# Two PSUM pairs kept through the late groups and the tail, single banks for the last chain, pieces of x W between the real and the imaginary products, ten units through GpSimd

## The chip, the cores and the metric

The kernel runs on one core of a Trainium2 chip. The core has TensorE (PE, matrix products, writing only to PSUM), VectorE (DVE) and ScalarE (ACT), which read PSUM and SBUF, GpSimd (POOL), which works on SBUF, and SyncE (SP), which here only issues DMAs. PSUM has eight banks of 2 KB per partition; one fp32 row of 512 fills a bank. The metric is the device time of one execution in microseconds (us); lower is better.

## The reference

Two layers in a row. The first is a linear attention with exponential features (8 batches, 8 heads, 576 tokens, 64 columns per head); its output, heads side by side, is x (8 x 576 x 512). The second mixes the lowest 64 frequencies of x along the sequence with complex weights for each frequency and ends in a product with w_ch:

```python
X = np.fft.rfft(x, axis=1)
Xr, Xi = (np.real(X[:, :n_modes]), np.imag(X[:, :n_modes]))
Yr = np.einsum('bmd,mde->bme', Xr, w_r) - np.einsum('bmd,mde->bme', Xi, w_i)
Yi = np.einsum('bmd,mde->bme', Xr, w_i) + np.einsum('bmd,mde->bme', Xi, w_r)
Y[:, :n_modes] = Yr + 1j * Yi
y = np.fft.irfft(Y, n=S, axis=1)
u = x + y
return (u + np.maximum(u @ w_ch, 0.0)).astype(np.float32)
```

w_r and w_i are 64 x 512 x 512 each in fp32, 134 MB together; they are read once.

## The kernel before, in words

**Stages.** The attention runs in steps n (the loop at L578). Beside it, and after it, the weights stream in: 32 groups k, each with a tile wr and a tile wi (128 x 8 x 512 in bf16, three buffers of each, tags w0 and w1), and each tile by two DMAs of 512 KB on POOL's queue (L166), which convert fp32 to bf16. A DMA for group k + 3 needs the buffer of group k, so POOL waits there for the matmuls that read it. mode_mm (L410) makes the product of one group with the spectrum XT, sixteen matmuls into psY: eight with wr, eight with wi. mode_sum (L443) adds psY to Yacc, and for the last eight groups, k = 24 to 31, writes the sum as yst in bf16.

**The late loop** (L834) covers k = 21 to 30, after the attention. Because u @ w_ch = x @ w_ch + y @ w_ch and y is an inverse transform (matrix CI) of Y, the kernel forms x @ w_ch ahead of time, "x W" below, in 17 pieces of two 128-token chunks: flip_x (L679) transposes two chunks into pt (PSUM tag tr) and copies them to sT on DVE; times_w (L690) does eight matmuls into psW (tag pW, two buffers), which ACT copies into xw. A group that has yst is transposed into ptY (tag tr) and copied into sY (transposed, L825). After every second such group by_batch (L734) multiplies sY by w_ch (mm_z) and by the identity (mm_r) into two psZY tiles of two banks each (tags T0, T1): z in the first bank, r in the second. Eight copies (four on ACT, four on DVE, L740) move these by batch into zall and yall; regroup(n) issues n pairs of them. reordered (L704) permutes chunk pairs of xs_all in place for "late" units, two matmuls and an ACT copy each, through T0 and T1. A table, plan (L831), says whether a second piece is done between the real and the imaginary product of a group; one piece always follows the imaginary product.

**The last group.** Here the PSUM pool psumL is closed and psumT opened (L870), with four pairs T0 to T3. Group 31's product goes to T1; unit 0's sums are started between its two halves; then come yst in two halves, two transposes and sY, mm_z and mm_r for h = 0 and h = 1 (T0, T1), and the move into rows 96 to 127 of zall and yall: batch 0 directly (L888, L889), the seven others through st (L893, L894) and DMAs on SP and POOL (L896).

**The units.** The output is made in 18 units of two chunks each, in the order of seq (L699): (batch, chunk, late). A unit adds x W and CI @ z in psB (add_xw L770, add_z L777), ACT takes its relu into the output tile o (L779), psA collects x and CI @ y (add_x L785, spec L791), and DVE adds psA to o (L793). A late unit leaves out the two matmuls for x; POOL adds x from xs_all instead (L796). Units with c = 4 are half units: they take the last chunk of four batches, and their two DMAs write from 64 partitions each, out of Yacc. The first and the last unit are cut in two. Even units use the pair T2, T3, odd ones T0, T1. SP issues the output DMAs (L916) in an order that is worked out from the list done (L899): a unit's number, for late ones a count of when POOL will be through. SP's queue runs in order, so a DMA that waits holds those behind it. An output tile takes a buffer of wr or wi.

All of this stands in manual_schedule blocks: on each engine the instructions run in the order of the program text.

Of the kernel before, what the change touches and what calls it, by code (L numbers as in the profile page):

```python
# [10 lines left out]
F32 = mybir.dt.float32  # L11
# [9 lines left out]
DMODEL = 512  # L21
# [5 lines left out]
def kernel(  # L27
# [639 lines left out]

    psum_cm = tc.tile_pool(name="psumL", bufs=1, space=bass.MemoryType.PSUM)
# [21 lines left out]
    def times_w():  # L690
        i, sT = ahead.pop(0)
        for x in range(2):
# [6 lines left out]
    seq = [(0, 0, 0), (0, 2, 1), (1, 0, 1), (1, 2, 1), (4, 0, 1), (4, 2, 1),  # L699
           (5, 0, 0), (5, 2, 1), (2, 0, 1), (0, 4, 0), (2, 2, 1), (6, 0, 1),  # L700
           (6, 2, 0), (3, 0, 1), (3, 2, 1), (2, 4, 0), (7, 0, 0), (7, 2, 0)]
    reorder = sorted(b * NCH + c for b, c, late in seq if late)

    def reordered(tag):  # L704
# [4 lines left out]
        ps = psum.tile([128, 2, DMODEL], F32, name="psX", tag=tag)  # L709
# [8 lines left out]
    def mm_z(ps, cols, h):  # L718
        for dc in range(4):
            for j in range(4):  # L720
                nc.tensor.matmul(ps[32 * j:32 * j + 32, 0, :], lhsT=cols[dc][:, j + 4 * h::8],
                                 rhs=wchb[:, dc, :], start=(dc == 0), stop=(dc == 3))

    def mm_r(ps, cols, h):
        for dc in range(4):
            for j in range(4):
                nc.tensor.matmul(
                    ps[32 * j:32 * j + 32, 1, dc * 128:(dc + 1) * 128],
                    lhsT=cols[dc][:, j + 4 * h::8], rhs=ident_b, start=True, stop=True)

    def zy_psum():
        return [psum.tile([128, 2, DMODEL], F32, name="psZY", tag=f"T{h}") for h in range(2)]

    def by_batch(sY, P):  # L734
        cols = columns(sY)
        ps = zy_psum()
        rows = slice(32 * P, 32 * P + 32)

# [3 lines left out]
        for h in range(2):  # L742
            mm_z(ps[h], cols, h)
            mm_r(ps[h], cols, h)
# [21 lines left out]
    def add_xw(u):  # L766
        u["psB"] = ps = psum.tile([128, 2, DMODEL], F32, name="psB", tag=u["tags"][0])
# [13 lines left out]
    def add_x(u):  # L781
        u["psA"] = ps = psum.tile([128, 2, DMODEL], F32, name="psA", tag=u["tags"][1])
# [17 lines left out]
    for n, (b, c, late) in enumerate(seq):  # L800
        u = dict(b=b, c=c, late=late == 1, half=c == 4, cut=n in (0, len(seq) - 1), n=n,
                 tags=("T2", "T3") if n % 2 == 0 else ("T0", "T1"))
# [28 lines left out]
    plan = {21: 2, 22: 2, 23: 2, 24: 2, 25: 1, 26: 2, 27: 1, 28: 1, 29: 1, 30: 2}  # L831
    with tc.manual_schedule():
        flip_x()
        for k in range(k_out, 31):  # L834
            gi = groups[k][1]
            while k_in < min(k + NW, 32):
                weights(k_in)
                k_in += 1
            issue_weights()
            psY = mode_mm(k, "pY", (0,))  # L840
            if plan[k] > 1:
                times_w()
                if todo:
                    flip_x()
            regroup(2)
            mode_mm(k, "pY", (1,), psY)
            yst = mode_sum(k, psY, pb)
            regroup(99)
            times_w()
# [5 lines left out]
            if todo:  # L855
                flip_x()
# [3 lines left out]
            if gi % 2 == 0 or k < 24:  # L860
# [3 lines left out]
        assert not todo and not copies  # L864
        while ahead:
            times_w()
        while reorder:
            reordered("T0")

    psum_cm.__exit__(None, None, None)  # L870
    psum = ctx.enter_context(tc.tile_pool(name="psumT", bufs=1, space=bass.MemoryType.PSUM))

    with tc.manual_schedule():
        psY = mode_mm(31, "T1", (0,))
# [3 lines left out]
        mode_mm(31, "T1", (1,), psY)  # L878
        yst = mode_sum(31, psY, pb)
        pt = psum.tile([128, 4, 128], BF16, name="ptY", tag="T0")  # L880
        transposed(yst, sY, 7, (((0, 2), pt[:, 0:2, :]), ((2, 4), pt[:, 2:4, :])))
        cols = columns(sY)
        ps = zy_psum()
        st = [pb.tile([128, 2, DMODEL], BF16, name=f"st{h}", bufs=1) for h in range(2)]
        rows = slice(96, 128)
        mm_z(ps[0], cols, 0)
        mm_r(ps[0], cols, 0)
        nc.scalar.copy(zall[rows, 0, :], ps[0][0:32, 0, :])  # L888
        nc.vector.tensor_copy(yall[rows, 0, :], ps[0][0:32, 1, :])  # L889
        mm_z(ps[1], cols, 1)  # L890
        mm_r(ps[1], cols, 1)
        for h in range(2):
            nc.scalar.copy(st[h][:, 0, :], ps[h][:, 0, :])  # L893
            nc.vector.tensor_copy(st[h][:, 1, :], ps[h][:, 1, :])  # L894
            for j in range(1 - h, 4):
                (nc.sync if j < 2 else nc.gpsimd).dma_start(  # L896
                    zy[rows, :, j + 4 * h, :], st[h][32 * j:32 * j + 32])

        done, free = [], 0  # L899
# [47 lines left out]
```

## Time and profile before

| | |
|---|---|
| time, median of 3 runs | 453.44 us (453.36 to 454.44) |
| the profiled execution | 454.95 us, its span 453.0 us |
| TensorE busy / weight loads | 309.5 us (68%) / 207.3 us (46%) |
| DVE, ACT, POOL busy | 300.7 us (66%), 273.0 us (60%), 221.0 us (49%) |
| HBM read / written | 163.64 MB / 9.44 MB |
| weight DMAs (POOL's queue) | 128 of 512 KB, median 18.6 and 19.0 us from issue to landing |
| output DMAs (SP's queue) | 14 of 512 KB, 8 of 256 KB, median 3.6 to 4.3 us |
| mean granted TensorE clock | 0.875 of full speed |

The shares are means over stages with different limits. The late loop runs from about 318 to 409 us, the last group's chain to 418, the units to 445, and the last output lands near 452. In a row of the timeline the columns are start, length, engine, line, operation, output <- input, shapes, count, and in brackets the idle time before it with what ended it. In a row of the windows they are the stretch, its length, the busy us of PE, PEld, DVE, ACT and POOL (count), the granted clock, the busy share of the 16 DMA engines (transfers that convert types count above 1) and GB/s.

### The profile page before, as it was taken

How to read it: one execution, taken by the hardware profiler on the slowest of the kernel's cores; microseconds unless marked ns; L12 is line 12 of the kernel's file. 1: busy time of each engine (PE TensorE's matmuls, PEld its weight loads, DVE VectorE, ACT ScalarE, POOL GpSimd, SP SyncE). 2: the span in 40 equal slices, each digit the busy share in tenths (PEclk: the TensorE clock that was granted, in tenths of full speed). 3: DMA queues.
4: the chain of work that ended last, by engine and by line, in shares of the span. 5: the costliest groups of instructions: out<-in, count | busy, mean ns of one | idle time of the engine just before them, and what ended most of it. 6: DMA issues, size and time to landing. Idle time of an engine off the chain costs nothing.

```text
span 453.0 us, 11872 instructions
## 1 busy us (share of the span) xinstructions
PE 309.5 (68%) x4979; PEld 207.3 (46%) x4997; DVE 300.7 (66%) x419; ACT 273.0 (60%) x570; POOL 221.0 (49%) x303
## 2 busy tenths in 40 slices
PE   3475677666566578666666577666999856677991
PEld 2364556555455466554454454444444424244440
DVE  6578879988599878988585587753222626263882
ACT  4575777767475588787575586662356625153761
POOL 3965557565565746644564464442232222100992
PEclk9997979988696668999698688887799989899998
DMA  6999999999999999999999999999999999990698
GB/s 177 208 229 219 207 192 218 227 218 218 206 232 221 223 232 220 222 228 221 222 232 212 221 234 211 211 211 211 211 211 211 211 211 211 211 189 15 228 351 298
DMA packets 60917, 97.83 MB, mean 216 GB/s; under 512 B 3904, under 2 KB 28800, under 8 KB 60864
## 3 DMA queue, kind: packets, MB, share of 16 engines
q0 software_dynamic: 51920, 76.75, 94.3%
q1 hardware_dynamic: 8784, 20.26, 13.1%
q8 instruction: 39, 0.64, 0.5%
q14 instruction: 14, 0.11, 0.1%
q10 hardware_dynamic: 160, 0.07, 0.1%
HBM read 163.64 MB, written 9.44 MB: 382 GB/s over the span
## 4 chain that ended last, share of the span: by engine, by line
DVE 27%; PE 26%; DMA 22%; ACT 9%; issue 6%; POOL 6%; SPq 1%; DVEq 0%; ACTq 0%; POOLq 0%
DMA wi<-in_moe_w_i_dram 21%; DVE mkq L245 9%; DVE xs_all L348 5%; DVE nd L334 4%; PE psW L695 3%; DVE tB L327 3%; ACT AA L252 3%; PE psNB L317 2%; PE ptr L196 2%; POOL vaug L282 2%; PE psY L435 2%; PE kvz L298 2%; ACT AA L256 2%; PE psB L770 2%; PE psWe L406 2%
## 5 line engine op out<-in xcount | busy, mean ns | idle before, releaser
L282 POOL TENSOR_TENSOR vaug<-vn,ee 128x576 bf16<-128x576 f32 x64 | 72.9, 1163 | 37.1 <-ACT ee L267 30.6
L166 POOL DMA_DIRECT2D wr<-in_moe_w_r_dram x48 | 29.7, 621 | 75.5 <-PE psY L435 30.0
L252 ACT ACTIVATE AA<-psT 128x1024 bf16<-128x1024 f32 x64 | 62.0, 1021 | 7.0 <-PE psT L220 6.3
L274 ACT ACTIVATE e<-mkq 64x4 f32<-64x4 f32 (+1 forms) x128 | 26.3, 206 | 65.4 <-DVE mkq L245 62.9
L256 ACT ACTIVATE AA<-psk 128x1024 bf16<-128x1024 f32 x64 | 61.3, 1008 | 0.0
L166 POOL DMA_DIRECT2D wi<-in_moe_w_i_dram x48 | 30.0, 628 | 35.8 <-DMA wi<-in_moe_w_i_dram 15.3
L202 DVE COPY kT<-ptr 128x640 bf16<-128x640 bf16 x32 | 15.7, 492 | 43.4 <-PE ptr L196 43.4
L298 PE MATMUL kvz<-vaug,AA 64*128 64x65 bf16 x1152 | 28.5, 207 | 22.0 <-POOL vaug L287 19.9
L697 ACT CAST xw<-psW 128x512 bf16<-128x512 f32 x34 | 19.8, 586 | 36.1 <-PE psW L695 31.8
L245 DVE TENSOR_REDUCE mkq<-psq 128x8 f32<-128x1024 f32 x32 | 38.9, 1217 | 0.8 <-PE psq L211 0.4
L245 DVE TENSOR_REDUCE mkq<-psk 128x8 f32<-128x1024 f32 x32 | 38.8, 1211 | 1.1 <-PE psk L211 1.0
L695 PE MATMUL psW<-wchb,sT 128*128 128x512 bf16 x126 | 35.4, 415 | 2.4 <-DVE sT L687 1.6
L298 PEld LDWEIGHTS <-AA 64*128 64x128 bf16 x1152 | 24.8, 105 | 26.1 <-issue 21.3
L348 DVE TENSOR_TENSOR xs_all<-nd,rden 128x640 bf16<-128x640 f32 x32 | 35.7, 1116 | 1.1
L220 PE MATMUL psT<-qT,w 64*128 64x512 bf16 x64 | 14.1, 428 | 31.6 <-DVE mkq L245 31.5
L317 PEld LDWEIGHTS <-AA 128*128 128x128 bf16 x640 | 31.5, 115 | 7.8 <-issue 7.4
L327 DVE TENSOR_TENSOR tB<-psNB,e 128x650 f32<-128x650 f32 x32 | 26.7, 833 | 9.7 <-PE psNB L317 8.9
L196 PE MATMUL ptr<-ident_b,k 128*128 128x128 bf16 x160 | 18.6, 265 | 16.8 <-DVE qT L202 14.8
L687 DVE COPY sT<-pt 128x1024 bf16<-128x1024 bf16 x17 | 11.8, 692 | 27.5 <-PE pt L684 23.6
L334 DVE TENSOR_TENSOR nd<-psNA,tB 128x650 f32<-128x650 f32 x32 | 26.7, 835 | 3.8 <-DVE tB L327 0.5
L435 PEld LDWEIGHTS <-XT 128*32 128x32 bf16 x384 | 15.0, 174 | 27.7 <-issue 14.3
L435 PE MATMUL psY<-wi,XT 128*32 128x512 bf16 x192 | 16.2, 408 | 11.2 <-DMA wi<-in_moe_w_i_dram 11.2
(136 smaller groups left out, 733.7 us busy)
## 6 DMA issues: line engine op xcount, KB each, us to landing
wr<-in_moe_w_r_dram POOLq DMA_DIRECT2D x64, 512.0 KB, 18.6
wi<-in_moe_w_i_dram POOLq DMA_DIRECT2D x64, 512.0 KB, 19.0
out_dram<-of SPq DMA_DIRECT2D x14, 512.0 KB, 4.1
vn<-in_v_dram SPq DMA_DIRECT2D x24, 288.0 KB, 6.2
q<-in_q_dram POOLq DMA_DIRECT2D x12, 288.0 KB, 18.0
k<-in_k_dram POOLq DMA_DIRECT2D x12, 288.0 KB, 16.2
vn<-in_v_dram SPq DMA_DIRECT2D x16, 144.0 KB, 4.8
out_dram<-of SPq DMA_DIRECT2D x4, 256.0 KB, 3.6
```

The source lines that it names most:

```text
L166: nc.gpsimd.dma_start(t.rearrange("p (m i) e -> p m (i e)", i=2), w[8 * gi + y:8 * gi + 8:2, g * 128:(g + 1) * 128, :].rearrange("m (p i) ...
L245: nc.vector.tensor_reduce(out=o, in_=i, axis=AX.X, op=ALU.max, apply_absolute_value=True)
L252: nc.scalar.activation(AA[:, 0, ab, 0:1024].rearrange("f (x j p) -> f j x p", j=2, p=64), st["psT"].rearrange("f j (x p) -> f j x p", p=64 ...
L256: nc.scalar.activation(AA[:, 1, ab, 0:1024].rearrange("p (c j f) -> p j c f", c=4, j=2), st["psk"], ACT.Exp, scale=sc)
L282: nc.gpsimd.tensor_tensor(out=vaug[:, ab, :, 0:64], in0=st["v"], in1=ee[:, ab, :].unsqueeze(2).to_broadcast([128, 9, D_]), op=ALU.mult,)
L298: nc.tensor.matmul(kvz[:, hh, ab * 65:(ab + 1) * 65], lhsT=AA[r, 1, ab, 128 * j:128 * j + 128], rhs=vaug[r, ab, j, :], start=(j == 0), sto ...
L317: nc.tensor.matmul(p[:, hh, 65 * c:65 * c + 65], lhsT=AA[:, 0, ab, x:x + 128], rhs=kvzF[:, hh, ab * 65:(ab + 1) * 65], start=True, stop=True,)
L327: nc.vector.tensor_tensor(out=tB, in0=st["psNB"], in1=e2.unsqueeze(3).to_broadcast([128, 2, NCH, 65]), op=ALU.mult,)
L334: nc.vector.tensor_tensor(out=nd, in0=st["psNA"], in1=st["tB"], op=ALU.add)
L348: nc.vector.tensor_tensor(out=xo, in0=nd[:, :, :, 0:64], in1=rden.to_broadcast([128, 2, NCH, 64]), op=ALU.mult,)
L435: nc.tensor.matmul(psY[32 * j:32 * j + 32, :], lhsT=XT[:, 16 + 32 * ri:48 + 32 * ri, 32 * i + 4 * gi + j], rhs=wt[ri][:, 2 * j + i, :], st ...
L695: nc.tensor.matmul(ps, lhsT=sT[:, x, dc, :], rhs=wchb[:, dc, :], start=(dc == 0), stop=(dc == 3))
```

## The change

Four things, all from the late loop on.

The pairs T0 and T1 move into a pool of their own, psumA, which is opened with psumL and stays open to the end. psumL then has the single banks tr, pY and two of pW. The close and reopen ahead of group 31 is gone; psumL is closed and psumT (T2, T3) opened ahead of unit 1. Even units use T0, T1 from psumA, odd ones T2, T3.

Group 31 takes its product in pY and its transposes in tr. Its z and r each get a tile of one bank: pW and pW for h = 0, pY and tr for h = 1. Batches 0 and 1 are moved directly (four copies instead of two), the other six by DMA.

In the late loop each group has a piece (times_w, then flip_x if any is left) between its real and its imaginary product, and all waiting copies of by_batch follow there. A second piece behind the imaginary product is done for k in pieces_behind.

seq has a new order with ten late units instead of eleven, and the order of the output DMAs counts 4 for a unit, 3 for a late one, 6 for a half one, and 5 for an add on POOL.

```diff
+    psumA = ctx.enter_context(tc.tile_pool(name="psumA", bufs=1, space=bass.MemoryType.PSUM))
     psum_cm = tc.tile_pool(name="psumL", bufs=1, space=bass.MemoryType.PSUM)
...
-    seq = [(0, 0, 0), (0, 2, 1), (1, 0, 1), (1, 2, 1), (4, 0, 1), (4, 2, 1),
-           (5, 0, 0), (5, 2, 1), (2, 0, 1), (0, 4, 0), (2, 2, 1), (6, 0, 1),
-           (6, 2, 0), (3, 0, 1), (3, 2, 1), (2, 4, 0), (7, 0, 0), (7, 2, 0)]
+    seq = [(0, 0, 0), (0, 2, 1), (1, 0, 1), (1, 2, 0), (2, 0, 1), (2, 2, 1),
+           (3, 0, 0), (3, 2, 1), (4, 0, 1), (0, 4, 0), (4, 2, 1), (5, 0, 1),
+           (5, 2, 0), (6, 0, 1), (6, 2, 1), (7, 0, 0), (2, 4, 0), (7, 2, 0)]
...
-                 tags=("T2", "T3") if n % 2 == 0 else ("T0", "T1"))
+                 tags=("T0", "T1") if n % 2 == 0 else ("T2", "T3"),
+                 pool=(lambda: psumA) if n % 2 == 0 else (lambda: psum))
...
-    plan = {21: 2, 22: 2, 23: 2, 24: 2, 25: 1, 26: 2, 27: 1, 28: 1, 29: 1, 30: 2}
+    def modes_of(k, part, psY=None):
+        if part == 0:
+            while issue["k"] < min(k + NW, 32):
+                weights(issue["k"])
+                issue["k"] += 1
+            issue_weights()
+        return mode_mm(k, "pY", (part,), psY)
+
+    def piece():
+        times_w()
+        if todo:
+            flip_x()
+
+    issue = dict(k=k_in)
+    pieces_behind = (21, 22, 24, 26, 28, 30)
...
-            psY = mode_mm(k, "pY", (0,))
-            if plan[k] > 1:
-                times_w()
-                if todo:
-                    flip_x()
-            regroup(2)
-            mode_mm(k, "pY", (1,), psY)
-            yst = mode_sum(k, psY, pb)
-            regroup(99)
-            times_w()
+            psY = modes_of(k, 0)
+            piece()
+            regroup(99)
+            modes_of(k, 1, psY)
+            yst = mode_sum(k, psY, pb)
+            if k in pieces_behind:
+                times_w()
...
-            if todo:
+            if k in pieces_behind and todo:
                 flip_x()
...
-    psum_cm.__exit__(None, None, None)
-    psum = ctx.enter_context(tc.tile_pool(name="psumT", bufs=1, space=bass.MemoryType.PSUM))
...
-        psY = mode_mm(31, "T1", (0,))
+        psY = modes_of(31, 0)
         u0 = units[0]
         add_xw(u0)
         add_x(u0)
-        mode_mm(31, "T1", (1,), psY)
+        modes_of(31, 1, psY)
...
-        mm_z(ps[0], cols, 0)
-        mm_r(ps[0], cols, 0)
-        nc.scalar.copy(zall[rows, 0, :], ps[0][0:32, 0, :])
-        nc.vector.tensor_copy(yall[rows, 0, :], ps[0][0:32, 1, :])
-        mm_z(ps[1], cols, 1)
-        mm_r(ps[1], cols, 1)
-        for h in range(2):
-            nc.scalar.copy(st[h][:, 0, :], ps[h][:, 0, :])
-            nc.vector.tensor_copy(st[h][:, 1, :], ps[h][:, 1, :])
-            for j in range(1 - h, 4):
-                (nc.sync if j < 2 else nc.gpsimd).dma_start(
+        for h, tags in ((0, ("pW", "pW")), (1, ("pY", "tr"))):
+            z, r = [psum.tile([128, DMODEL], F32, name="ps" + "ZR"[x], tag=tags[x],
+                              bufs=2 if h == 0 else 1) for x in range(2)]
+            mm_z(z, cols, h)
+            mm_r(r, cols, h)
+            for j in range(2 - 2 * h):
+                nc.scalar.copy(zall[rows, j, :], z[32 * j:32 * j + 32])
+                nc.vector.tensor_copy(yall[rows, j, :], r[32 * j:32 * j + 32])
+            nc.scalar.copy(st[h][:, 0, :], z)
+            nc.vector.tensor_copy(st[h][:, 1, :], r)
+            for j in range(2 - 2 * h, 4):
+                (nc.sync if j % 2 == 0 else nc.gpsimd).dma_start(
                     zy[rows, :, j + 4 * h, :], st[h][32 * j:32 * j + 32])
...
-            free = max(free, 2 * n) + 3 if u["late"] else free
-            done.append((free if u["late"] else 2 * n, n))
+            t += 6 if u["half"] else 3 if u["late"] else 4
+            if u["late"]:
+                free = max(free, t) + 5
+            u["t"] = t
+            at_end.append((free if u["late"] else t, n))
...
+            if n == 1:
+                psum_cm.__exit__(None, None, None)
+                psum = ctx.enter_context(
+                    tc.tile_pool(name="psumT", bufs=1, space=bass.MemoryType.PSUM))
```

## The prediction

> **What bounds the kernel now.** I read the page's slices first, then the DMA issues and one-microsecond windows around 410 us, the chain of waits, the timeline from 409 us on, and the output stage in windows. Times of the trace are us from the start of the span, which is 453.0 in the profiled execution.
>
> The page's slices (DMA, then GB/s), the two DMA issues that matter, and windows around the last weight's landing:
>
> ```profile
> DMA  6999999999999999999999999999999999990698
> GB/s 177 208 229 219 207 192 218 227 218 218 206 232 221 223 232 220 222 228 221 222 232 212 221 234 211 211 211 211 211 211 211 211 211 211 211 189 15 228 351 298
> ...
> 390.43 0.61 POOL L166 DMA_DIRECT2D wi<-in_moe_w_i_dram  x1 [1.63 <-DMA wi<-in_moe_w_i_dram]
> ...
> wi<-in_moe_w_i_dram POOLq DMA_DIRECT2D x2, 512.0 KB, 19.5
> ...
> 409.00:410.00 1.00, 0.27 (x5) 0.35 (x8) 0.00 (x0) 0.58 (x1) 0.00 (x0) 1.00 0.09 16
> 410.00:411.00 1.00, 1.00 (x12) 0.31 (x4) 0.00 (x0) 0.00 (x0) 0.00 (x0) 1.00 0.00 0
> ```
>
> The weight stream is full from slice 2 to the last weight. The last piece is issued at 390.43 and lands some 19.5 later, at 410.0, and nothing moves after it. So nothing the change does to TensorE before that can pay unless it reaches the work behind 410.0. That work, from the timeline:
>
> ```profile
> 409.73 0.67 PE L435 MATMUL psY<-wr,XT 128*32 128x512 bf16 x8 [0.89 <-ACT xw L697]
> 411.30 0.69 PE L435 MATMUL psY<-wi,XT 128*32 128x512 bf16 x8
> ...
> 413.90 1.09 PE L721 MATMUL psZY<-wchb,sY 128*32 128x512 bf16 x16 [0.38 <-DVE sY L829]
> ...
> 415.32 0.57 ACT L888 CAST zy<-psZY 32x512 bf16<-32x512 f32 x1 [5.64 <-PE psZY L727]
> ...
> 415.92 0.68 DVE L889 CAST zy<-psZY 32x512 bf16<-32x512 f32 x1 [2.08 <-ACT zy L888]
> 416.64 1.07 ACT L893 CAST st<-psZY 128x512 bf16<-128x512 f32 x2 [0.75 <-DVE zy L889]
> ...
> 418.01 0.61 PE L770 MATMUL psB<-xw,ident_p 128*128 128x512 bf16 x2 [0.70 <-DVE st L894]
> ...
> 421.45 23.05 POOL L796 TENSOR_TENSOR of<-of,xs_all 128x1024 f32<-128x1024 f32 x11 [0.65 <-DVE of L793]
> ```
>
> Two delays are seen. The last imaginary product starts 1.27 after its weight landed, since PSUM is handed from one pool to the next (0.89 for ACT's last xw copy) and unit 0's sums stand ahead of it. And ACT and DVE take turns on psZY, each waiting for the other. The output stage, in windows (last two columns: share of the DMA engines, GB/s):
>
> ```profile
> 424.00:430.00 6.00, 5.95 (x31) 2.66 (x32) 5.29 (x5) 4.48 (x5) 6.00 (x4) 1.00 0.61 244
> 430.00:434.00 4.00, 4.00 (x27) 1.78 (x24) 3.13 (x4) 2.53 (x4) 4.00 (x3) 1.00 0.95 374
> 434.00:438.00 4.00, 4.00 (x20) 1.76 (x18) 3.31 (x4) 2.75 (x4) 4.00 (x3) 1.00 0.97 268
> 438.00:442.00 4.00, 3.85 (x26) 1.80 (x26) 3.45 (x3) 2.75 (x3) 4.00 (x3) 1.00 1.03 420
> 446.00:450.00 4.00, 0.00 (x0) 0.00 (x0) 0.00 (x0) 0.00 (x0) 0.00 (x0) 0.85 1.02 402
> ```
>
> TensorE is full to 443.8, POOL to 444.5, but the DMA share is already 0.95 to 1.03 from 430 on and stays so when all engines are idle. The end (last issue 447.77, landing 4.0 later, span end 1.2 after) is set by the output transfers; what they lost, they lost before 430, at 0.5 to 0.6, because the five units behind unit 0 are all late and POOL gives one per 2.13.
>
> **Part 1, pieces of x W moved between the products.** No instruction is added. A piece (eight psW matmuls and two ACT copies of 0.585; with the next flip, eight pt transposes and a DVE copy of 0.69) leaves the place behind the imaginary product for k = 23, 25, 27, 29 and stands ahead of it for k = 25, 27, 28, 29. For k = 29 the trace has TensorE waiting 3.98 for the weight, then 3.5 for eight psW matmuls at clock 0.5. Moved into that wait they cost nothing (without it, 1.90 + 0.61 each). Behind 390.19 remain: psY .7, yst .7, ptY .4, sY .42, so psZY starts near 392.6 instead of 395.65. Then k = 30: its real weight lands at 395.1 (issue 375.23 + 19.9): psY .67, piece 1.90, flip .61, to 398.2; imaginary product at its landing, 400.1 (380.20 + 19.9). DVE does two zy casts to 397.4, sT at 398.3, two more zy casts (1.23 each) to 401.5, yst to 402.2 (404.8 now). Piece to 402.7, ptY, sY, flip and sT to 404.95, last piece to 406.85, real product of k = 31 (landed 385.45 + 19.6 = 405) to 407.5. That is 2.9 earlier than now (410.4), but unit 0's four matmuls (0.97) end at 408.5 and TensorE then waits for the weight at 410.0. So 1.6 is slack, and **the gain of parts 1 and 2 ahead of the last product is 411.30 − 410.08 = 1.22**, no more.
>
> The pieces delay the release of the wi buffers, on which POOL's weight issues wait. Behind them on POOL's queue there is only the next weight. Issue to landing is 19.5 here, so a release may come late by many us before the stream has a hole; I cost it at nothing.
>
> **Part 2, PSUM.** The hand-over ahead of k = 31 goes away (in the 1.22); a new one stands ahead of unit 1, which must wait until the four single banks are read; behind it on TensorE stand all other units. Now unit 1 waits for st too. With z and r in tiles of their own, ACT and DVE no longer take turns. From psZY at 413.90 − 1.22 = 412.68: z is read from +1.14 (ACT: 2 × 0.58 for zall, then st, 0.59 each, to 416.2); r is ready at +1.4, and DVE, the longer string, does 0.68 + 0.69 + 0.69 + 0.69 with 0.02 between: 416.9. Two of these eight copies are new (zall and yall of j = 1, 0.57 and 0.68); they replace one zy DMA, so six remain on SP and POOL, issued from 416.3 to 418.2 and landed (2.2) by 420.6, while the first unit that needs one (b = 2, unit 4) comes at 421. Unit 1 starts at **416.95 instead of 418.01, 1.06 earlier**. The trace doesn't show how a new pool waits on these banks: at best for the first two (416.2, 0.75 more gain), at worst as in the third rival.
>
> **Part 3, order of units and ten late ones.** Per unit TensorE takes 6 × 0.216 = 1.30 if late, 1.73 if not, 1.85 for a half one (timeline). One late less adds 0.43: units 1 to 17 take 10 × 1.30 + 5 × 1.73 + 2 × 1.85 = 25.35, to 442.3. One POOL add (2.13) goes. A unit leaves DVE about 1.9 behind its last matmul (ACT 1.02, DVE 1.225), a late one 2.2 later from POOL. With two late ones to one other, POOL no longer falls behind: outputs are ready at 422.5 (n1), 422.9 (n3), 424.6 (n2), 426.8 (n4), 427.3 (n6), 428.9 (n5), 431.2 (n7), and so on to 443.8 (n17); the order on SP's queue follows this, so nothing waits behind a unit that isn't ready.
>
> Transfers: a lone one lands 3.0 after its issue, so I take 1.7 to start and 1.28 of service (512 KB at some 410 GB/s, windows at 420 and 402), 0.65 for half of a cut unit, and 1.17 for each half-unit transfer, as 319 GB/s from 442 to 446 suggests. Before, this sum with the trace's issue rules ends at 451.2 (the trace: 451.8). After: n1 lands 425.5, n3 426.8, n2 428.0, n4 429.8, n6 431.1, n5 432.4, n7 434.1, n9 436.5, n8 437.8, n10 439.0, n12 440.3, n11 441.6, n13 442.9, n15 444.2, n14 445.5, n16 447.8, n17 449.1. **Difference 2.05**: 1.06 of start, 1.0 from fewer holes. Holes of only 0.5 + 0.5 are left behind 425, so the transfers set the end, and TensorE, done at 442.3, doesn't.
>
> Sum: 453.0 − 2.05 = 450.95 for a profiled span; the timed median, 0.44 above the span, becomes 453.44 − 2.05 = **451.4**. Least credible gain 0.5 (third rival), largest: 0.75 for the pool and 0.75 if holes and the half units' slow transfers close, so 449.9.
>
> **The clock.** The granted clock falls on little work. Windows of 3.41:
>
> ```profile
> 308.89:312.30 3.41, 1.20 (x17) 0.69 (x12) 2.38 (x5) 0.73 (x2) 0.61 (x1) 1.00 1.12 212
> 312.30:315.71 3.41, 2.13 (x26) 1.46 (x24) 0.41 (x1) 1.32 (x3) 0.00 (x0) 0.50 1.12 211
> 404.46:407.87 3.41, 1.72 (x16) 1.07 (x17) 1.45 (x3) 0.00 (x0) 0.00 (x0) 1.00 0.70 130
> ```
>
> A window 35% busy is followed by clock 0.5, one 50% busy isn't. After the change TensorE has 0.97 to 1.5 of work in a window that begins between 407.5 and 409.7. The Trainium skill ("TensorE: Matmul & The Clock Gate", Why this matters for your kernels) asks only that gaps stay under about 3 us; by that rule the gaps of 1.6 would be harmless and the sum stays 451.4. The first rows above speak against it.
>
> **Rivals.** 1: *half clock over the last chain*, for the reason just given, where the window begins in the bad stretch. psZY (2.4 of matmuls) and the transposes double for up to 3.4: r of h = 1 comes 1.0 to 1.6 later and so does unit 1. For it: the rows; against: where a window begins is not fixed, and if an earlier one (397.5 to 400.9) falls too, the slack of 1.6 is used and the later one is full. 451.4 + 1.2 = 452.6. Chance 0.17.
> 2: *engines, not transfers, bound the new end*: if the half units' slow transfers don't recur, the end is the last issue (444.3) + 3.4 + 1.2 = 448.9 in the span, 449.4. Against: 0.95 to 1.03 shares. Chance 0.10.
> 3: *single banks don't part ACT and DVE*: the turns go on, with one turn more: 413.82 + 2 × (0.60 + 0.72) + 0.62 + 2 × 0.70 = 418.5, unit 1 is 0.5 later than now, and the order's 1.0 remains: 452.9. Against: zy casts of two psZY tiles overlap at 398 (ACT 1.00, DVE 1.22). Chance 0.06.
> 4, slower: *a hole in the weight stream*. Pieces ahead of the imaginary product hold wi. It decides once a release comes so late that a weight issued at once lands behind its turn: issue to landing takes 8.4 where the queue is short (at 180 us), 11.3 at worst in this stage (k = 24, 326.0) and 19.6 from 346 on, so there are some 3 us to spare at k = 24 and 11 later. Two lost slots (512 KB at 211 GB/s, 2.5 each) cost 5.0: 456.4. Against: at k = 24 both kernels run the same order. Chance 0.05.
>
> **Chances.** Forecast 0.62, with 450.6 to 452.1 of its own. 0.3% is 1.4 us, what a measurement can tell from no change: faster means under 452.1. Faster: 0.57 + 0.10 = 0.67; within: 0.05 + 0.16 + 0.05 = 0.26; slower: 0.07, rival 4 and 0.01 each of rivals 1 and 3. The range 449.9 to 452.9 leaves out half of rival 2 and rival 4 and some tails.
>
> **What would show it.** Right: wi of k = 31 starts within 0.1 of its landing, no wait for ACT xw ahead of psY; ACT and DVE copies of Z and R overlap; unit 1 starts 4.3 behind psZY; POOL's ten adds have gaps; DMA share over 0.9 from 424 on. Wrong: clock 0.5 between 410 and 418; DVE waiting for ACT in the copies; SP's queue idle while POOL is ahead of it; a GB/s row under 205 before 400.

## The result, and the profile after

The changed kernel takes 452.37 us (median of 10 runs, 451.15 to 454.14); the kernel before, run beside it, 454.56 (10 runs, 453.36 to 456.01). The ratio is 0.995, with a 95% interval of 0.9931 to 0.997: 2.2 us less, where 2.05 were forecast. The level came out 1.0 above the forecast of 451.4 because the three times of the kernel before that the forecast started from (median 453.44) are low among its ten. The profiled execution of the changed kernel is the slowest of its ten runs: 454.14 us, span 452.2. In all ten the time is 1.9 to 2.1 above the span. So this trace shows how the parts lie, and also something that not every run has.

The page of the kernel after, the rows of its 40 slices for the granted clock, the DMA share and GB/s:

```profile
PEclk9996969988688679996599678988699997998997
DMA  6999999999999999999999999999999999991697
GB/s 177 199 229 214 201 190 217 218 221 219 213 231 221 222 234 219 232 223 221 222 222 221 222 234 211 211 211 211 211 211 212 210 211 211 211 201 32 231 358 283
```

The weight stream is as whole as before: 210 to 212 GB/s in every slice from the 25th to the 35th, no hole. The last weight lands at 410.76 here (410.03 before). What changed lies behind it: GB/s of 32, 231, 358 and 283 in the last four slices, where before they were 15, 228, 351 and 298.

The timeline of the kernel after, around the last group (rows of TensorE, ACT and DVE; start and length first):

```profile
410.81 0.69 PE L435 MATMUL psY<-wi,XT 128*32 128x512 bf16 x8 [1.69 <-DMA wi<-in_moe_w_i_dram]
...
413.00 1.93 PE L722 MATMUL psZ<-wchb,sY 128*32 128x512 bf16 x16
...
414.99 1.18 ACT L891 CAST zy<-psZ 32x512 bf16<-32x512 f32 x2 [6.84 <-PE psZ L722]
...
415.42 1.40 DVE L892 CAST zy<-psR 32x512 bf16<-32x512 f32 x2 [2.02 <-PE psR L728]
...
416.83 1.29 DVE L894 CAST st<-psR 128x512 bf16<-128x512 f32 x2
...
418.17 0.61 PE L768 MATMUL psB<-xw,ident_p 128*128 128x512 bf16 x2 [0.32 <-DVE st L894]
```

The last imaginary product starts 0.04 behind its landing and has waited 1.69 for it: this is the slack. ACT and DVE copy at the same time (414.99 to 416.17 against 415.42 to 416.82), neither waits for the other. But sixteen z matmuls take 1.93, where the sixteen of before took 1.09, and unit 1 starts 5.17 behind the first of them. The reason is in the windows of the kernel after (stretch, length, busy us of PE, PEld, DVE, ACT, POOL, granted clock, DMA share, GB/s):

```profile
409.25:412.67 3.42, 0.98 (x10) 0.47 (x11) 1.05 (x3) 0.00 (x0) 0.00 (x0) 1.00 0.15 28
412.67:416.08 3.41, 3.38 (x46) 1.66 (x49) 0.96 (x2) 1.07 (x2) 0.00 (x0) 0.50 0.02 5
...
424.00:430.00 6.00, 6.00 (x32) 2.65 (x32) 4.86 (x5) 4.49 (x5) 5.96 (x3) 1.00 0.79 313
430.00:434.00 4.00, 4.00 (x27) 1.80 (x24) 3.13 (x4) 2.53 (x4) 3.91 (x3) 1.00 0.91 358
...
438.00:442.00 4.00, 4.00 (x27) 1.66 (x26) 3.52 (x3) 2.86 (x3) 3.86 (x3) 1.00 1.02 410
```

A window with 0.98 of work in 3.42 is followed by one at clock 0.5, and that one holds the z matmuls. This is the first rival's event. In the output stage the DMA share is now 0.79 instead of 0.61 from 424 to 430, as the new order was to bring about.

To compare kernels, each profile is cut into four terms behind the landing of the last weight: the wait of the imaginary product, from there to the first z matmul, from there to unit 1, and from unit 1 to the landing of the last output (the span ends 1.2 later).

| kernel | ratio to before (95%) | wait of wi | to z | to unit 1 | to last landing | sum |
|---|---|---|---|---|---|---|
| before | 1 | 1.27 | 2.60 | 4.11 | 33.75 | 41.73 |
| after | 0.995 (0.9931, 0.997) | 0.04 | 2.19 | 5.17 | 32.77 | 40.17 |
| e1_filler | 0.9948 (0.9932, 0.9964) | 0.82 | 2.09 | 4.17 | 32.67 | 39.75 |
| e2_halves_by_batch | 1.0307 (1.0289, 1.0324) | 0.04 | 2.09 | 4.17 | 49.26 | 55.56 |
| e3_pieces_back | 0.9953 (0.9934, 0.9971) | 0.39 | 2.10 | 4.17 | 32.76 | 39.42 |
| e4_order_alone | 0.999 (0.9978, 1.0002) | 2.71 | 2.59 | 4.12 | 33.12 | 42.54 |
| e5_parts_1_2 | 0.9964 (0.9945, 0.9982) | 0.04 | 2.09 | 4.88 | 33.32 | 40.33 |
| e6_two_pools | 0.9923 (0.991, 0.9935) | 0.04 | 2.09 | 3.66 | 32.97 | 38.76 |
| e7_filler_with_room | 0.994 (0.9927, 0.9954) | 0.04 | 2.09 | 4.16 | 32.61 | 38.90 |
| e8_two_outputs_out | 0.9948 (0.9933, 0.9962) | 0.04 | 2.19 | 5.17 | 32.82 | 40.22 |
| e9_banks_alone | 0.9985 (0.9969, 1.0001) | 0.35 | 2.08 | 4.16 | 33.76 | 40.35 |
| e10_room_and_pools | 0.9921 (0.9891, 0.995) | 0.04 | 2.08 | 3.66 | 32.59 | 38.37 |
| e11_halves_early | 0.9906 (0.9879, 0.9932) | 0.04 | 2.09 | 3.66 | 32.00 | 37.79 |
| e12_changed_again | 0.9942 (0.9921, 0.9963) | 0.58 | 2.08 | 4.16 | 32.64 | 39.46 |

One profile stands for one execution. e5 and e9, whose units and output DMAs are the same, differ by 0.44 in the last term, so a few tenths there say little. The landing itself lies between 408.2 and 410.8 in these profiles, with the same stream of weights in each, so a time holds that too; the terms are read from profiles, the verdicts from the ratios.

### The profile page after: what moved, and what is told of

The parts are those of the page before. It is cut to its first block, busy times and chain, and to the rows that moved or that the text cites. A ratio compares the mean times of both kernels' runs of the same rounds, so it can differ in the third digit from the quotient of the medians.

```text
span 452.2 us, 11896 instructions
## 1 busy us (share of the span) xinstructions
PE 314.2 (69%) x4997; PEld 207.8 (46%) x4997; DVE 299.1 (66%) x420; ACT 273.2 (60%) x570; POOL 218.0 (48%) x301
## 4 chain that ended last, share of the span: by engine, by line
DMA 32%; PE 23%; DVE 20%; ACT 9%; issue 6%; POOL 6%; SPq 1%; DVEq 0%; ACTq 0%; POOLq 0%
DMA wi<-in_moe_w_i_dram 26%; DVE mkq L245 6%; DMA wr<-in_moe_w_r_dram 4%; DVE xs_all L348 4%; DVE nd L334 3%; ACT AA L252 3%; POOL vaug L282 3%; DVE tB L327 2%; PE psWe L406 2%; ACT AA L256 2%; PE psNB L317 2%; PE kvz L298 2%; PE psY L435 2%; PE psB L768 2%; PE psB L775 2%
## 5 line engine op out<-in xcount | busy, mean ns | idle before, releaser
L696 PE MATMUL psW<-wchb,sT 128*128 128x512 bf16 x136 | 33.4, 390 | 1.5 <-DVE sT L688 1.5
L348 DVE TENSOR_TENSOR xs_all<-nd,rden 128x640 bf16<-128x640 f32 x32 | 33.2, 1038 | 1.1
L307 ACT CAST kvzF<-kvz 128x260 bf16<-128x260 f32 x32 | 12.2, 380 | 20.1 <-PE kvz L298 20.0
```

The lines of the kernel that those rows point to most:

```text
L348: nc.vector.tensor_tensor(out=xo, in0=nd[:, :, :, 0:64], in1=rden.to_broadcast([128, 2, NCH, 64]), op=ALU.mult,)
L696: nc.tensor.matmul(ps, lhsT=sT[:, x, dc, :], rhs=wchb[:, dc, :], start=(dc == 0), stop=(dc == 3))
```

## The experiments

### The granted clock: e1_filler, e7_filler_with_room, e12_changed_again

The first rival came true in the profiled run. Is it always there, and what does it cost? e1 gives TensorE matmuls whose result nobody reads, ahead of the last two products and between product and z.

```diff
+    def filler(n, tag="pW"):
+        pf = psum.tile([128, DMODEL], F32, name="psF", tag=tag, bufs=2)
+        for _ in range(n):
+            nc.tensor.matmul(pf, lhsT=ident_b, rhs=wchb[:, 0, :], start=True, stop=True)
...
             piece()
+            if k == 30:
+                filler(7)
...
         add_x(u0)
+        filler(6)
         modes_of(31, 1, psY)
+        filler(2)
```

> The changed kernel with idle matmuls added while TensorE waits for a weight: 7 ahead of the imaginary product of k = 30, 6 ahead of that of k = 31, 2 behind it (0.216 each, into a free pW bank, never read). Theory (half clock over the last chain cost the changed kernel's profile about 1): every window of 3.41 from 395 on is over half busy, the granted clock stays 1.0 until the units end, the sixteen z matmuls of h = 0 take 1.1 instead of 1.93, unit 1 starts 6.2 to 6.5 after the last weight's landing instead of 7.4; time 0.3 to 1.0 below the changed kernel's 0.995 of before, so 0.993. Rival (the transfers set the end whatever the chain does): unit 1 comes earlier, but the end behind the last landing stays at 41.4 and the ratio at 0.995. Rival (matmuls that nobody reads cost): ratio over 0.996.

The chain kept clock 1.0 (4.17 from z to unit 1), but the product came 0.82 late and the ratio is that of the changed kernel, not the 0.993 expected. The windows of e1 show why:

```profile
390.20:393.61 3.41, 2.11 (x24) 0.88 (x20) 1.12 (x2) 0.00 (x0) 0.48 (x1) 0.50 1.12 211
393.61:397.02 3.41, 3.41 (x64) 1.87 (x60) 0.00 (x0) 2.00 (x2) 0.00 (x0) 0.50 1.12 211
```

In this run the clock was 0.5 for two windows earlier, from 390.2 on. That used up the slack; the seven fillers at 399.68 and the six at 409.48 (1.67 and 1.46 us) then stood ahead of the last products. So a filler of fixed length is a remedy where there is slack and a delay where an earlier slow window has used it up. e7 makes room first (a piece goes from behind k = 30 to behind k = 23) and then fills more:

```diff
-    pieces_behind = (21, 22, 24, 26, 28, 30)
+    pieces_behind = (21, 22, 23, 24, 26, 28)
...
+            if k == 30:
+                filler(7)
...
+        filler(10)
         modes_of(31, 1, psY)
+        filler(2)
```

> The changed kernel with idle matmuls in TensorE's waits (7 ahead of the imaginary product of k = 30, 10 ahead of that of k = 31, 2 behind it, never read) and with room for them: the second piece of k = 30 is done at k = 23 instead. Theory (the clock, by where its windows begin, costs the chain up to 1 in part of the runs): the imaginary product of k = 31 starts within 0.1 of its landing, the clock is 1.0 from 400 on, unit 1 starts 6.2 to 6.4 behind the landing; median 0.4 to 0.8 below the changed kernel's, ratio 0.9935 to 0.994, and slowest minus fastest run under 2. Rival (the spread of the runs comes from ahead of the late loop): ratio 0.995, spread 2 to 3 as in the changed kernel.

e7 takes 452.32 (451.06 to 452.51), ratio 0.994. The timeline of e7 (TensorE):

```profile
406.74 2.32 PE L846 MATMUL psF<-wchb,ident_b 128*128 128x512 bf16 x10
410.14 0.68 PE L435 MATMUL psY<-wi,XT 128*32 128x512 bf16 x8 [1.07 <-DMA wi<-in_moe_w_i_dram]
...
412.23 1.11 PE L722 MATMUL psZ<-wchb,sY 128*32 128x512 bf16 x16
...
416.39 0.60 PE L768 MATMUL psB<-xw,ident_p 128*128 128x512 bf16 x2 [0.73 <-DVE st L903]
```

The windows of e7 ahead of that product:

```profile
404.30:407.70 3.40, 2.47 (x17) 1.16 (x18) 0.00 (x0) 0.58 (x1) 0.00 (x0) 1.00 0.74 139
407.70:411.10 3.40, 2.33 (x17) 0.78 (x15) 0.22 (x1) 0.00 (x0) 0.00 (x0) 1.00 0.23 43
```

With 2.3 to 2.5 of work in each window the clock stays at 1.0 from 377 to the end of the units. The product still waits 1.07 for its weight, so the fillers delay nothing, and z to unit 1 is 4.16. The spread is 1.45 us over six runs; the changed kernel has 3.0 over ten, but e1, whose fillers ran into a slow window, has 1.72 over six, so it isn't shown that the spread fell because of the clock. The median hardly moves against the changed kernel, as one would expect if only part of that one's runs have the slow window over the chain. e12 is the changed kernel once more, with a profile of its own.

> The changed kernel as it is, beside the three above on one chip: ratio 0.995, unit 1 between 6.2 and 7.4 behind the last landing by where the clock's windows begin, last landing 32.6 to 32.8 behind unit 1.

It took 451.61 (450.75 to 452.96). This profile has clock 0.5 at 390.6 and at 404.2 to 407.6, not over the chain: wi is 0.58 late and z to unit 1 takes 4.16. So the slow window moves from run to run, and over the chain it costs 5.17 − 4.16 = 1.0 us plus 0.1 ahead of z. The old chain can lose by it too: in e4, below, 1.44.

### Which part brought what: e3, e4, e5, e9

e3 puts the pieces of x W back to where they were (the old plan of counts, a piece between the products only where the plan says two) and leaves the rest.

```diff
-            piece()
+            if plan[k] > 1:
+                piece()
...
-    pieces_behind = (21, 22, 24, 26, 28, 30)
+    pieces_behind = range(21, 31)
```

> The changed kernel with the pieces of x W where they were (a piece always behind the imaginary product, a second one between the products by the old table). Theory (the moved pieces gave the slack of 1.6 ahead of the last product, of which the removed hand-over needs only part): the last piece, the real product and unit 0's four matmuls end near or behind the last landing, the imaginary product of k = 31 starts 0.5 to 0.8 behind its landing instead of 0.05, ratio 0.996. Rival (moving the pieces did nothing, the hand-over alone gave the 1.22): it starts within 0.1 of its landing, ratio 0.995.

wi starts 0.39 behind its landing instead of 0.04 and the time is 452.52, ratio 0.9953: the same within the intervals. In these profiles the pieces are worth a few tenths; the rest of the 1.22 comes from the hand-over of PSUM that is gone. e4 is the other end: the kernel before with the new order of units alone.

```diff
-    seq = [(0, 0, 0), (0, 2, 1), (1, 0, 1), (1, 2, 1), (4, 0, 1), (4, 2, 1),
...
+    seq = [(0, 0, 0), (0, 2, 1), (1, 0, 1), (1, 2, 0), (2, 0, 1), (2, 2, 1),
...
```

> The kernel before with part 3 alone: the new order of units with ten late ones, and the new order of output DMAs; PSUM pools and pieces as before. Theory (the order gives 1.0 by filling the output transfers' holes): unit 1 starts 8.0 behind the last landing as before, DMA share from 424 to 430 rises from 0.61 to about 0.8, the end behind the last landing falls from 43.0 by 1.0, ratio 0.998. Rival (the order gives all of it): ratio 0.995. Rival (nothing, the gain is all in the chain ahead of unit 1): ratio 1.000.

From unit 1 to the last landing it takes 33.12 instead of 33.75, and the ratio is 0.999 (0.9978 to 1.0002). The timeline of e4 (TensorE) shows the old hand-over at its worst:

```profile
406.59 3.16 PE L695 MATMUL psW<-wchb,sT 128*128 128x512 bf16 x7 [0.79 <-DVE sT L687]
410.85 0.67 PE L435 MATMUL psY<-wr,XT 128*32 128x512 bf16 x8 [1.10 <-ACT xw L697]
...
412.42 0.68 PE L435 MATMUL psY<-wi,XT 128*32 128x512 bf16 x8
...
421.41 0.59 PE L777 MATMUL psB<-zy,CI 128*128 128x512 bf16 x2 [0.38 <-DMA zy<-st]
```

Here a slow window fell on the last piece (406.6 to 410.0 at clock 0.5: 3.16 for seven matmuls). The real product waits for the piece and for ACT's copy, so wi comes 2.71 behind its landing instead of 1.27. What the changed kernel has ahead of the landing is some 1.7 of room, which takes up part of such a window: in e12, with clock 0.5 from 404.2 to 407.6, the product was 0.58 late.

The last row is unit 2, which waits 0.38 for a DMA of z; the kernel before has the same wait (0.37). The changed kernel copies batch 1 directly and has none, which fits the 0.35 between e4's 33.12 and its 32.77. If so, that much belongs to part 2, as long as TensorE's pace bounds the tail (see e8); no run tests it by itself.

e5 has the pieces and the banks, with the old order; e9 has the banks alone, with the old order and, as in e3, the old pieces. In e3 and e9 all waiting copies of by_batch still follow ahead of the imaginary product, as in the changed kernel. The diff is that of e5, without the order of the output DMAs.

```diff
-    seq = [(0, 0, 0), (0, 2, 1), (1, 0, 1), (1, 2, 0), (2, 0, 1), (2, 2, 1),
...
+    seq = [(0, 0, 0), (0, 2, 1), (1, 0, 1), (1, 2, 1), (4, 0, 1), (4, 2, 1),
...
```

> The changed kernel with part 3 undone: the old order of units with eleven late ones and the old order of output DMAs; PSUM pools and pieces as changed. Theory (the chain ahead of unit 1 and the order each give their own part): unit 1 starts 6.3 (clock 1.0) to 7.4 (clock 0.5) behind the last weight's landing as in the changed kernel, and the last output lands 33.4 to 33.8 behind unit 1 as before, instead of 32.7; ratio to before 0.997. Rival (the order is worth nothing, as its 0.999 alone may also be read): 32.7 stays, ratio 0.995. Rival (the order is all): ratio 1.000.

> Part 2 alone: the kernel before with the changed PSUM pools and the single banks of the last chain; pieces, units and output DMAs in the old order. Theory (part 2 holds nearly all of the chain's gain, the pieces a few tenths): imaginary product of k = 31 0.3 to 0.7 behind its landing (1.27 before), first z matmul 2.1 behind it (2.6 before), unit 1 6.6 to 7.6 behind the landing, tail from unit 1 33.3; ratio 0.9965 to 0.9975. Rival (without the moved pieces the last product is as late as before): 1.2 behind its landing, ratio 0.999.

e5: 452.87, ratio 0.9964, and its profile again has the slow window over the chain (4.88). e9: 453.52, ratio 0.9985, where 0.9965 to 0.9975 were expected. The timeline of e9 (TensorE):

```profile
410.32 0.68 PE L435 MATMUL psY<-wi,XT 128*32 128x512 bf16 x8
412.40 1.11 PE L722 MATMUL psZ<-wchb,sY 128*32 128x512 bf16 x16
...
416.57 0.60 PE L768 MATMUL psB<-xw,ident_p 128*128 128x512 bf16 x2 [0.74 <-DVE st L896]
```

The banks alone bring wi to 0.35 and shorten the way to z from 2.60 to 2.08; from z to unit 1 they bring nothing (4.16 against 4.11). In times (one less the ratio, of some 454.7): order alone 0.5 us of 454.7, banks alone 0.7, pieces and banks 1.6, banks and order 2.1, all three 2.3 to 2.6. Each has an interval of 0.5 to 1.0 to either side, so how the parts add up isn't settled (the pieces come out at 0.9 by e5 and e9, and at 0.1 to 0.5 by the changed kernel and e3); none of them is seen to cost anything.

### What unit 1 waits for: e6_two_pools

In the kernel before, unit 1 followed the first of DVE's two st copies, in the changed kernel it follows the second (the two end 0.65 apart). That is why z to unit 1 has stayed at 4.1 to 4.2 though the copies no longer take turns. e6 divides psumL in two, so that T2, unit 1's first tile, waits for the banks of h = 0 alone.

```diff
-    psum_cm = tc.tile_pool(name="psumL", bufs=1, space=bass.MemoryType.PSUM)
-    psum = psum_cm.__enter__()
+    psumR_cm = tc.tile_pool(name="psumR", bufs=1, space=bass.MemoryType.PSUM)
+    psumR = psumR_cm.__enter__()
+    psumW_cm = tc.tile_pool(name="psumW", bufs=1, space=bass.MemoryType.PSUM)
+    psumW = psumW_cm.__enter__()
+    class psum:
+        @staticmethod
+        def tile(*a, tag, **kw):
+            return (psumW if tag in ("pW", "T2") else psumR).tile(*a, tag=tag, **kw)
...
-                psum_cm.__exit__(None, None, None)
+                psumW_cm.__exit__(None, None, None)
+                psumR_cm.__exit__(None, None, None)
+                psumR = ctx.enter_context(
+                    tc.tile_pool(name="psumT3", bufs=1, space=bass.MemoryType.PSUM))
+                psumW = ctx.enter_context(
+                    tc.tile_pool(name="psumT2", bufs=1, space=bass.MemoryType.PSUM))
```

The pool with T3 takes the place of pY and tr (z and r of h = 1), the one with T2 that of the two pW (h = 0).

> The changed kernel with the four single banks in two pools, so that unit 1's first pair needs only the two banks of h = 0 read, and its second pair the two of h = 1. Theory (unit 1's start carries the whole tail with it): unit 1 starts 3.4 to 3.6 behind the first z matmul instead of 4.17, the last landing stays 32.7 behind unit 1, so the end comes 0.6 to 0.7 earlier, ratio 0.9935. Rival (unit 1's second sum then waits 0.7 for h = 1, and nothing is won behind it): the last landing moves to 33.3 behind unit 1, ratio 0.995.

z to unit 1 falls to 3.66 and the ratio to 0.9923 (451.28 us, 450.65 to 451.96). The timeline of e6 (TensorE):

```profile
412.10 1.11 PE L729 MATMUL psZ<-wchb,sY 128*32 128x512 bf16 x16
...
415.76 0.59 PE L775 MATMUL psB<-xw,ident_p 128*128 128x512 bf16 x2 [0.22 <-DVE st L901]
```

The wait for DVE's st is now the one for h = 0 and costs 0.22, and 0.5 of the 0.75 that the prediction held possible for this was there to be had. It is not shown by e6 that a new pool waits for all banks of the closed one: in the changed kernel T2 itself lies on the banks that tr and pY had, which hold r and z of h = 1, and in e6 on those of h = 0, so a wait for its own two banks would give the same. For the pool as a whole speaks the old hand-over: there group 31's product lay on the bank that tr had, and it still waited 0.89 for ACT's copy out of pW. The changed kernel with T2 and T3 exchanged would tell; it was not run.

### What sets the end: e8_two_outputs_out, e2_halves_by_batch

The prediction said that the transfers set the end from 425 on. e8 leaves out the two transfers of units 3 and 6.

```diff
-                for dst, src in units[at_end.pop(0)[1]]["dmas"]:
+                m = at_end.pop(0)[1]
+                for dst, src in units[m]["dmas"] if m not in (3, 6) else ():
```

> The changed kernel without the output DMAs of units 3 and 6 (512 KB each; those two parts of the output are not written), all else as it is. Theory (from 425 on the output transfers set the end): the last landing comes 2.5 earlier, 30.0 to 30.5 behind unit 1 instead of 32.7; ratio to before 0.989 to 0.990. Rival (engines and the issue of the last DMA set it): it stays at 32.4 to 32.8, ratio 0.995.

Nothing follows from it: 452.55, ratio 0.9948, and from unit 1 to the last landing 32.82 against 32.77. The windows of e8, set 1.68 earlier than those of the kernel after, since its unit 1 starts that much earlier (416.49):

```profile
422.32:428.32 6.00, 5.95 (x31) 2.64 (x32) 4.86 (x5) 4.48 (x5) 5.96 (x3) 1.00 0.56 227
428.32:432.32 4.00, 4.00 (x27) 1.80 (x24) 3.13 (x4) 2.53 (x4) 3.91 (x3) 1.00 0.58 229
432.32:436.32 4.00, 3.95 (x19) 1.81 (x19) 3.31 (x4) 2.78 (x3) 3.68 (x3) 1.00 1.00 311
```

The queue is emptier (0.56 and 0.58 instead of 0.79 and 0.91), the end isn't earlier. The DMA issues of the kernel after, window 441.0 to 441.5, hold one transfer, that of unit 13 (KB, median us from issue to landing):

```profile
out_dram<-of SPq DMA_DIRECT2D x1, 512.0 KB, 3.1
```

3.1 is close to what a lone transfer takes (3.0 in the prediction; 3.2 for unit 13's in e8). So a share of 1.02 from 438 to 442 was a queue just kept busy, with hardly a backlog at unit 13. What is late is the unit. POOL and, in the last row, DVE in the timeline of the kernel after:

```profile
421.67 12.80 POOL L794 TENSOR_TENSOR of<-of,xs_all 128x1024 f32<-128x1024 f32 x6 [1.69 <-DVE of L791]
434.79 8.59 POOL L794 TENSOR_TENSOR of<-of,xs_all 128x1024 f32<-128x1024 f32 x4 [0.32 <-DVE of L791]
...
439.15 2.13 POOL L794 TENSOR_TENSOR of<-of,xs_all 128x1024 f32<-128x1024 f32 x1
...
437.85 1.22 DVE L791 TENSOR_TENSOR of<-psA,of 128x1024 f32<-128x1024 f32 x1 [0.55 <-DMA out_dram<-Yacc]
```

Ten adds of 2.14 with small gaps, the largest 0.32. The ninth is unit 13's, from 439.15 to 441.28, and the transfer is issued at 441.31. The add starts 0.08 behind the end of DVE's for the same unit (437.85 + 1.22), while POOL had been free for 0.14: it is TensorE's pace (4.00 of 4.00 in the windows above) that sets when unit 13 is ready, and POOL adds its 2.13. POOL alone would be nearly as late. Behind it come 2 MB more in six transfers (units 15 and 14, two halves of 16, two of 17), which last from its landing at 444.40 to 450.94. The end is thus set by unit 1's start, the pace of TensorE up to unit 13, that unit's add on POOL, and the six transfers behind. In the kernel before there was a backlog: the eight 512 KB transfers issued from 428.4 to 441 have a median of 4.2 there.

Among those six are the two of unit 16, a half unit, 256 KB each, at 4.6 from issue to landing. e2 tries to have them faster by cutting a half unit by batch instead of by halves of the partitions, so that each transfer reads all 128 partitions, with a target whose outermost dimension counts 2.

```diff
-                (bass.AP(tensor=out.tensor, offset=out.offset + ((b + 4 * y) * S_ + 4) * DMODEL,
-                          ap=[[9 * DMODEL, 64], [S_ * DMODEL, 2], [1, DMODEL]]),
-                  o[64 * y:64 * y + 64]) for y in range(2)]
+                (bass.AP(tensor=out.tensor, offset=out.offset + ((b + x) * S_ + 4) * DMODEL,
+                          ap=[[4 * S_ * DMODEL, 2], [9 * DMODEL, 64], [1, DMODEL]]),
+                  o[:, x, :]) for x in range(2)]
```

> The changed kernel with the two DMAs of a half unit cut by batch (128 partitions, one 2 KB row each) instead of by partition half (64 partitions, two 2 KB rows each); same bytes, same number of descriptors. Theory (transfers set the end, and those from 64 partitions are slow): a half unit's pair takes 1.3 to 1.5 of the DMA engines instead of 2.3 to 2.9, the end comes 1 to 2 earlier behind the last weight's landing than in the changed kernel (41.4), ratio to before 0.991 to 0.993. Rival (engines set the end, or the slow part is the 2 KB rows and not the 64 partitions): the pair still takes over 2.2, or it gets shorter and the end stays; ratio 0.995.

It is a loss: 468.19, ratio 1.0307, 16 us above the changed kernel. The windows of e2:

```profile
420.00:430.00 10.00, 9.95 (x54) 4.43 (x54) 8.49 (x8) 6.58 (x8) 9.88 (x6) 1.00 0.76 302
430.00:440.00 10.00, 9.95 (x54) 4.36 (x53) 8.02 (x8) 7.02 (x7) 9.56 (x5) 1.00 0.55 197
```

The DMA view of e2, 430 to 470, in slices of 1 us:

```profile
GB/s 229 393 156 20 39 49 53 303 373 356 360 356 381 414 420 397 356 61 53 53 53 49 53 49 53 49 315 244 53 51 51 51 51 51 25 0 0 8 0 0
```

TensorE and POOL are at work as before, but the DMA share from 430 to 440 is 0.55. Behind a half unit's issue (430.5 and 444.7) the flow falls to 49 to 53 GB/s for many slices of 1 us. At a share of 1.02 the 16 engines move 410 (438 to 442, kernel after), some 25 each, so this is two of them. The Trainium skill ("DMA: Bandwidth & Descriptors", Rules for kernel authors) says that an outermost dimension below 16 confines a transfer to as many engines, and this run agrees. Whether it is the 64 partitions that make the old half units slow was thereby not tested and stays open.

### Together: e10_room_and_pools, e11_halves_early

e10 is e7 with the two pools of e6. e11 is e10 with the half units as units 7 and 11 instead of 9 and 16, and nine late units.

```diff
+    seq = [(0, 0, 0), (0, 2, 1), (1, 0, 1), (1, 2, 0), (2, 0, 1), (2, 2, 1),
+           (3, 0, 0), (0, 4, 0), (3, 2, 1), (4, 0, 1), (4, 2, 0), (2, 4, 0),
+           (5, 0, 1), (5, 2, 1), (6, 0, 0), (6, 2, 1), (7, 0, 0), (7, 2, 0)]
```

> The changed kernel with both improvements: filler with room, and two pools for the single banks. Theory (their gains lie at different places and add): unit 1 5.6 to 5.8 behind the last landing at clock 1.0, tail 32.6 to 33.0, ratio 0.991 to 0.992, all runs within 2. Rival (the two pools' gain was one lucky phase of the clock): ratio 0.994 as with the filler alone.

> As the run with room and two pools, with another order: nine late units, the half units at places 7 and 11 instead of 9 and 16, (7, 0) and (7, 2) plain at the end. Theory (the end is unit 13's output, whose transfer finds the queue empty, and the five transfers behind it, two of them the slow ones from 64 partitions; put earlier they fall into holes): the last landing comes 0.4 to 0.6 earlier behind unit 1 (32.1 to 32.4), ratio 0.990 to 0.991. Rival (the end is TensorE's pace, and one late unit less costs it 0.43): the last landing 33.0 or later behind unit 1, ratio 0.992 or above.

e10: 450.58 (449.63 to 451.5), ratio 0.9921. By terms it is e6 with the clock held up, but its ratio is that of e6 alone (0.9923), so the times don't show that the two gains add. e11: 449.90 (449.42 to 451.43), ratio 0.9906 (0.9879 to 0.9932), the lowest median of all, 4.2 below the kernel before in the same job (454.1); its interval overlaps those of e10 and e6. The windows of e11, set 3.45 earlier than those of the kernel after, as its unit 1 is (414.72):

```profile
420.55:426.55 6.00, 6.00 (x36) 2.60 (x35) 4.70 (x5) 3.83 (x5) 5.96 (x3) 1.00 0.79 313
426.55:430.55 4.00, 4.00 (x23) 1.75 (x23) 3.28 (x4) 2.89 (x3) 1.95 (x2) 1.00 1.01 369
```

The first window is that of the kernel after (0.79). In the second, with the first half unit in it, POOL is down to 1.95 of 4 and the DMA share is 1.01 instead of 0.91. The last half unit's transfers are issued at 433.6, with seven others behind them. From unit 1 to the last landing it takes 32.00 instead of 32.6, though TensorE has 0.4 more to do, so the rival fell. How much is due to the place of the half units and how much to the ninth late unit was not parted.

## Why the prediction was right, point by point

**The size** was right, 2.2 measured for 2.05, in part by luck: what the forecast missed ahead of z (0.5, below) and what the slow window takes in part of the runs (1.1) pull in opposite ways. As single profiles have it, the four terms behind the landing give 41.73 − 40.17 = 1.56 in the profiled run with the slow window over the chain, 41.73 − 39.46 = 2.27 in e12, and 41.73 − 38.90 = 2.83 with the clock held up (e7).

**Parts 1 and 2 ahead of the product, 1.22.** Right: the wait fell from 1.27 to 0.04, with 1.69 of slack where 1.6 was worked out. Most of it is due to PSUM (0.92 of it comes with the banks alone, e9), a few tenths to the pieces; the prediction did not part the two. That the pieces cost the weight stream nothing is confirmed by the rows of 210 to 212 GB/s; the fourth rival has nothing for it.

**From product to unit 1, 1.06 in total (1.22 from the earlier product, less 0.16 for a longer chain).** Too small, and one mechanism was missed. With the clock at 1.0, the sum of wait, way to z and way to unit 1 falls from 7.98 to 6.29, by 1.69. The missed step lies ahead of z: 2.60 became 2.09. Before, psZY took the tag of ptY and its first matmul waited 0.38 for the second sY copy; with a bank of its own it starts after the first copy. The prediction took psZY's start as the product's plus 2.60. From z to unit 1 it forecast 4.27 (4.11 before), and 4.16 came. The copies by ACT and DVE do run side by side, so the third rival fell; but the time won was spent on the wait for the banks of h = 1 too, where unit 1 before had waited for those of h = 0 (3.66 with two pools, e6).

**The order, 1.0.** Right in the profile of the changed kernel (33.75 to 32.77). In e4 it is 0.6; the other 0.35 fits unit 2's wait for z, which the direct copy of batch 1 takes away. In times the order is 0.5 by itself, with an interval that just holds no change.

**The transfers set the end from 425 on.** This sentence failed, though the sum beside it held: unit 13 lands 441.31 + 3.1, as the sum has it if unit 1's later start (418.17 for 416.95) is added to its 442.9. The sum itself has no backlog at unit 13. The share of 0.95 to 1.03 was rightly read as one in the kernel before (median 4.2 from issue to landing), but with the new order hardly any is left at unit 13. e8 shows that 1 MB less changes nothing. Of the signs named for this, the DMA share over 0.9 from 424 on didn't come (0.79 up to 430), and POOL's gaps are small (0.32 at most): TensorE and POOL keep nearly the same pace, and TensorE's, the slower by some 0.1, sets when unit 13 is ready.

**The second rival** (engines bound the end) is right as to the place up to unit 13 and wrong as to the price, since the six transfers behind still take 6.5 (444.40 to 450.94).

**The first rival** (half clock) had the mechanism and the price right, 1.0 to 1.1 in the profiled run for 1.2 forecast; as a forecast of the median it fails. Of the eight profiles with the new banks and no filler the slow window lies over the chain in three (after, e5, e8); how often it does in the runs that were only timed is open.

## What to carry to other kernels

A DMA share near 1 doesn't say that transfers bound the end: look whether a transfer lands as fast as a lone one, and if so, ask which engine released it late. Where a PSUM pool is replaced by another, look which reads of the old pool's banks the new one's first tile waits for, and divide the pool along what is free first. In a stretch that waits for a weight, leave room and put work into it, in this order: filler without room is only another delay in the phases where the slow clock came earlier.

## What the runs showed of the hardware

A wait of only 1.69 us was followed by half clock; the window of 3.41 around it held 0.98 of work, and windows with 2.3 to 2.5 kept the clock. The changes of the granted clock within a profile lie a whole number of such windows apart, in all fourteen profiles. Cut into these windows from 295 to 442 us, the profiles hold 52 falls from full clock and 431 windows that kept it. The busiest window before a fall held 1.59 of work (e5), the least busy one that kept the clock 1.46 (the kernel after), so here it is decided between 42 and 47% busy. Two windows at that edge, one from e5, followed by clock 0.5, and the one from the kernel after, followed by 1.0:

```profile
407.91:411.33 3.42, 1.58 (x20) 0.77 (x20) 1.34 (x4) 0.00 (x0) 0.00 (x0) 1.00 0.02 4
...
399.01:402.43 3.42, 1.46 (x12) 0.65 (x12) 3.34 (x4) 2.12 (x3) 0.00 (x0) 1.00 1.12 211
```

The Trainium skill ("TensorE: Matmul & The Clock Gate", Part 1) calls this window free-running, which agrees: in the same kernel the clock fell at 412.7 in one run and at 404.2 in another. By the rule of the Trainium skill ("TensorE: Matmul & The Clock Gate", Why this matters for your kernels) on gaps over about 3 us this wait would have been harmless; here the measurement decides.

A transfer whose target has an outermost dimension of 2 moved at 49 to 53 GB/s, an eighth of the 410 of the others (e2).
